# A longer planned latency for the loads of the weight preparation, a wider spread of it, queries' low parts on partitions 0 to 63, and sinks' probabilities moved by small transfers

## The chip, the core and the metric

The kernel runs on one core of a Trainium2 chip. The metric is the time of one execution in microseconds (us). The profile is of one execution and names the engines so: PE is TensorE (PEld its weight loads), DVE is VectorE, ACT is ScalarE, POOL is GpSimd, SP is SyncE, whose queue (SPq) issues nearly all DMAs here. L12 is line 12 of the kernel before.

## What is computed

Sliding-window attention with sink keys, then two feed-forward layers without gating. Everything is float32; a product is made of two or three passes of a faster format on a high and a low part of each number.

```
scores = (1/sqrt(64)) * q @ k.T                 # 4 x 8 heads, 768 positions, 64 wide
keep   = (key < 4) | (0 <= query - key < 128)   # 4 sink keys, a window of 128
a = softmax(where(keep, scores, -1e9));  x = a @ v          # -> 3072 tokens x 512
h = relu(x @ moe_w_in);                  x = (h*h) @ moe_w_out      # 512 -> 2048 -> 512
h = x @ moe2_w_in;  g = h - tanh(h);     out = g @ moe2_w_out
```

## The kernel before

**Tiling and stages.** Attention is done in jobs, one for a head and a block of 384 queries: 8 blocks of 8 heads. The first 16 jobs are done in plain float32 (`plain`), the other 48 in split form (`job`, `scores`, `values`). Layer one (`step1`) runs over 8 token blocks `t` of 384 and 16 slices `n` of the hidden width: `mm_a` makes a slice in bank `ph` or `T`, ReLU and square follow (`r`), a high and a low part (`gh`, `gl`) are made, and `mm_b` adds the slice's share to the four banks `acc`. While layer one works on a block, the attention of the next but one is done between its matmuls. Layer two (`pair2`, `step2`) starts when layer one is over, at about 690 us, and needs its weights in a prepared form.

**The weight preparation** is the third thing that runs beside layer one. `sums` (16 items) and `halves` (16 items) prepare the weights of layer two for later: each loads a piece of `w` into the one buffer `zr`, rebuilds float32 from 64-bit words in the buffer `wd` (`to_single`: rebias L586 on ACT or L588 on DVE, then L591, L593, L595 on DVE), subtracts pieces (L626, L629), splits into a high part (back into `zr`) and a low part (L289, `wd<-wd,zr`), and stores both to DRAM (`wc`, or `wo` for `halves`). The next item's load of `zr` waits for the store of this one. `SUMS` says at which point of layer one, in token blocks, each of the 32 items is due: from 2.0 at steps of 0.13.

**One split job on the engines.** PE makes scores of 128 queries in bank `S` (L345 with the keys' high part, L346 with the low), three times a job; DVE lays the causal half over it (L350) and takes the row's minimum (L411, which frees `S`), ACT takes the exponential (L355). The probabilities are normed (`cb`), those of the sinks split into `ask`, and PE transposes all into bank `O` (L379 three times, L380 for `ask`: for the three groups of queries, 8 rows each stand on partitions 0, 32 and 64). ACT copies the transposed window part to `xe` (high), DVE subtracts (L391, low), POOL cuts it to the window by two selects (L395, `pt`); three small copies of 8x128 bring the sinks' rows from bank `O` to partitions 0 to 7 of `pts`. Then PE multiplies with the values (L431, L434 with `pt`, and last L436 with `pts`), into the same bank `O`; `tmp` and `x` (copy, L447, L449) take the result out.

**Low parts of queries.** The queries of a head stand twice in `raw` and in `qq`, on partitions 0 to 63 and again on 64 to 127 (so do the keys). A copy makes both halves of `qq` high parts; a subtraction (L289, `qq<-raw,qq`, 64x384) then turns the half on partitions 64 to 127 into low parts.

**What sets the order.** No engine's order is written out. Every operation is given to `Order` with the engines that can do it, a cost on each (`C(occupied, took)`; `c_act`, `c_two` and so on), a priority (its due time) and what it reads and writes. `solve` plans all of them, DMAs too (engine `D`, planned in `load` with bytes / 300 ns or at least 430 ns, and 1700 ns until the data are there), and the operations are written down by their planned starts. Each engine then works through its list in that order; an operation whose input is late holds up all that stand behind it on that engine, and SP's queue does likewise. A fixed number of completion semaphores for DMAs is used in turn.

Of the kernel before, what the change touches and what calls it, by code (L numbers as in the profile page):

```python
# [12 lines left out]
F32 = mybir.dt.float32  # L13
F32R = mybir.dt.float32r
# [26 lines left out]

EARLY = 25.0, 8.0
RING = 9
SUMS = tuple(2.0 + i * 0.13 for i in range(32))
LATER = 190.0
NU = NM // 2
NC = 7
REBIAS = 2.0 ** -112
# [185 lines left out]
def c_two(n, psum=False):  # L234

    return C(n / 0.96 + 72, None, not psum)
# [4 lines left out]
    return {"A": c_act(n, psum), "V": c_one(n, psum or apart)}  # L241


def c_pool(n):
    return C(max(2.35 * n + 110, 290.0), None, True)

# [11 lines left out]
class Fast:  # L258
# [30 lines left out]
            (nc.vector if e == "V" else nc.gpsimd).tensor_tensor(out=out, in0=a, in1=b.bitcast(F32), op=ALU.subtract)  # L289
        self.o.add({"V": c_two(n), "P": c_pool(n)}, prio, reads, writes, emit)  # L290

    def load(self, prio, writes, get, nbytes, reads=()):
        nc = self.nc

        def emit(e):
            out, in_ = get()
            nc.sync.dma_start(out=out, in_=in_)
        t = max(nbytes / 300.0, 430.0)
        self.o.add({"D": C(t, t + 1700.0)}, prio, reads, writes, emit)


    def job(self, j, due):

        t = self.t
        blk, head = divmod(j, H)
        b, half = divmod(blk, 2)
        plain = j < PLAIN
        nk, nv, k2 = KW[half], NV[half] - 2 * (not plain), j % 2
        q, r = (j % 4, j % 4) if plain else (k2, k2)
        d = due[0]  # L310
        if j > 1:
            src, early = self.raw[half][b * H + head], 8 * plain
            self.load(d - 24 - early, [("rq", q), ("rk", q)], lambda: (t["raw", q][:, :QW[half]], src[:, :QW[half]]), P * QW[half] * 4)
            self.load(d - 23 - early, [("rv", r)], lambda: (t["rv", r][:, :nv * D], src[:, RW[half] - nv * D:]), P * nv * D * 4)

        def vals():
            return t["rv", r][:, :nv * D].rearrange("p (n d) -> p n d", d=D)
        if plain:
            self.plain(j, half, head, blk, q, due)
            return  # L320
        x = t["raw", q]
        self.copy(d - 16, [("rq", q)], [("qh", k2), ("ql", k2)], lambda: (t["qq", k2], x[:, :N1]), N1)
        self.sub(d - 15, [("rq", q)], [("ql", k2)], lambda: (t["qq", k2][64:], x[64:, :N1], t["qq", k2][64:]), N1)
        self.copy(d - 16, [("rk", q)], [("kh", k2)], lambda: (t["kh", k2][:, :nk], x[:, N1:N1 + nk]), nk)
        self.sub(d - 15, [("rk", q), ("kh", k2)], [("kl", k2)], lambda: (t["kl", k2][:, :nk], x[:, N1:N1 + nk], t["kh", k2][:, :nk]), nk)
        vh, vl = (slice(D, 2 * D), slice(0, D)) if head % 2 == 0 else (slice(0, D), slice(D, 2 * D))
        self.copy(d - 8, [("rv", r)], [("vh", k2)], lambda: (t["vv", k2][:, :nv, vh], vals()), nv * D, apart=True)
        self.sub(d - 7, [("rv", r), ("vh", k2)], [("vl", k2)], lambda: (t["vv", k2][:, :nv, vl], vals(), t["vv", k2][:, :nv, vh]), nv * D)
        self.scores(j, half, due)
        self.values(j, half, head, blk, due[2])  # L330

    def scores(self, j, half, due):
# [59 lines left out]
        for s, sign, op in ((1, 1, ALU.is_ge), (0, -1, ALU.is_gt)):  # L392
            u = 0 if s else i0
            o.add({"P": c_sel(2 * P * (3 - u))}, d - 5, [(*xe, 0), (*xe, 1)], [("pt", 2 * i + s) for i in range(u, 3)],
                  lambda e, u=u, s=s, sign=sign, op=op: nc.gpsimd.affine_select(  # L395
                      out=t[pt].rearrange("p (n t) q -> p n t q", t=2)[:, 2 * u:, s, :], in_=t[xe][:, 2 * u:, :].bitcast(F32),
                      pattern=[[0, 2 * (3 - u)], [sign, P]], compare_op=op, fill=0.0, base=0, channel_multiplier=-sign))
        for i in range(3):
            self.copy(d - 6, [tb], [("pts", k2, i)], lambda i=i: (t["pts", k2][0:8, i * P:(i + 1) * P], bank[tb][32 * i:32 * i + 8, 3 * P:]), P, True)

    @staticmethod
    def keys(half, i):
# [17 lines left out]
    def values(self, j, half, head, blk, d):  # L420
        nc, o, t, bank = self.nc, self.o, self.t, self.bank
        k2, ob = j % 2, ("O", 0)
        wins = self.windows(half)


        def pv(e):
            oo, vv, pt, pts = bank[ob], t["vv", k2], t["pt", 0], t["pts", k2]
            for n, (b, sl, cnt, c) in enumerate(wins):
                k = sl + sl // 2 * 2
                if sl == 5:  # L430
                    nc.tensor.matmul(out=oo[:, c:c + 2 * P], lhsT=vv[:, b - 2, :], rhs=pt[:, k:k + 3:2, :], start=False, stop=False)  # L431
                    continue
                for l in range(2):
                    nc.tensor.matmul(out=oo[:, c:c + cnt * P], lhsT=vv[:, b - 2, :], rhs=pt[:, k + 2 * l:k + 2 * l + 3 * cnt - 2:3, :],  # L434
                                     start=(n == 0 and l == 0), stop=False)
            nc.tensor.matmul(out=oo[:, :N1], lhsT=vv[:, 0, :], rhs=pts, start=False, stop=True)  # L436
        o.add({"T": c_mm(N1, *[256] * (5 + 2 * half))}, d - 4,
              [("vh", k2), ("vl", k2)] + [("pts", k2, i) for i in range(3)] + [("pt", s) for s in range(1 - half, 6)], [ob], pv)

        r, q = (0, 64) if head % 2 == 0 else (64, 0)  # L440

        def at(x, w):
            return t[x, 0][r:r + 64, w]
        own, one, low = slice(0, N1), slice(2 * P, N1), slice(N1, N1 + P)
        self.copy(d - 3, [ob], [("tmp", 0)], lambda: (at("tmp", slice(0, 512)), bank[ob][q:q + 64, :]), 512, True)
        o.add({"V": c_two(N1, True)}, d - 2.5, [ob, ("tmp", 0)], [("x", r)],
              lambda e: nc.vector.tensor_tensor(out=at("x", own), in0=bank[ob][r:r + 64, :N1], in1=at("tmp", own), op=ALU.add))  # L447
        o.add({"V": c_two(P), "P": c_pool(P)}, d - 2.4, [("tmp", 0), ("x", r)], [("x", r)],
              lambda e: (nc.vector if e == "V" else nc.gpsimd).tensor_tensor(out=at("x", one), in0=at("x", one), in1=at("tmp", low), op=ALU.add))  # L449
        self.split(head, blk, d, ("x", 0), [("x", 0), ("x", 64)])  # L450

# [158 lines left out]
    def sums(self, u, kc, prio, after):  # L610
# [7 lines left out]
        rk, zk = ("zr", 0), [("wd", 0), ("wd", 1)]  # L618
        for m, dst in ((u + NU, slice(0, 4, 3)), (u, slice(1, 3))):
            self.load(prio - 6, [(*rk, m // NU)],  # L620
                      lambda m=m, dst=dst: (four[:, dst, :], self.w[1][m, :, :1024].rearrange("p (n c) -> p n c", c=2 * P)[:, kc:4:2, :]), P * 2048, after)
        rks = [(*rk, 0), (*rk, 1)]
        self.to_single(prio, lambda: (raw, z[:, :512]), rks, zk)
        tt = nc.vector.tensor_tensor
# [15 lines left out]
    def halves(self, n, prio, after):  # L640


        raw, z = self.t["zr", 0], self.t["wd", 0]
        rks, zk = [("zr", 0, 0), ("zr", 0, 1)], [("wd", 0), ("wd", 1)]
        m, zf = n // 2 + (1 - n % 2) * NU, z[:, :512].bitcast(F32)
        self.load(prio - 6, rks, lambda: (raw, self.w[1][m, :, 1024:]), P * 4096, after)
        self.to_single(prio, lambda: (raw, z[:, :512]), rks, zk)
        hi, lo = raw[:, :512].bitcast(F32R), z[:, :512].bitcast(F32R)
        self.copy(prio + 0.6, zk, rks, lambda: (hi, zf), 512)
        self.sub(prio + 0.7, zk + rks, zk, lambda: (lo, zf, hi), 512)  # L650
        for i, (src, ks) in enumerate(((hi, rks), (lo, zk))):
            self.load(prio + 0.8, [("wo", n, i)], lambda i=i, src=src: (self.wo[:, n, i * 512:(i + 1) * 512], src.bitcast(F32)), P * 2048, ks)
# [204 lines left out]
    def plan(self):  # L857
# [16 lines left out]
                due = [base(blk) + u * span(blk) - 2.0 for u in us]  # L874
                self.job(blk * H + head, due)

        attn = {"qh", "ql", "kh", "kl", "vh", "vl", "cb", "nm", "ss", "rs", "ask", "xe", "pt", "pts", "tmp", "x"}
        own = [(x, i) for x in ("qh", "ql", "kh", "kl", "vh", "vl", "ss", "rs", "tmp") for i in range(2)] + [("pt", i) for i in range(6)] + [("x", 0), ("x", 64)]
        own += [(x, k, i) for x in ("cb", "nm", "ss", "ask", "xe", "pts") for k in range(2) for i in range(3)]
        attention(0)  # L880
        self.switch(lambda k: k[0] == "wide", [("acc", i) for i in range(4)] + [("ph", 0), ("S", 0)], self.x_wide, self.banks)
# [8 lines left out]
        for q in range(4):  # L890
# [2 lines left out]
                            own, self.x_plain, self.attn)  # L893
            for n in range(8):
                self.step1(q % 2, n + 8 * (q // 2), PV[q] + n * PS[q], q // 2)
            if q > 1:
                attention(q)
        for t in range(2, NB1):
# [32 lines left out]
        for t in range(NB2):  # L931
# [4 lines left out]

    ATTN = (("qq", 2, (N1,), F32R), ("kh", 2, (KW[1],), F32R), ("kl", 2, (KW[1],), F32R), ("vv", 2, (NV[1] - 2, 2 * D), F32R),
            ("cb", 2, (3, 132), F32), ("nm", 2, (3,), F32), ("ss", 2, (3,), F32), ("rs", 2, (3,), F32), ("ask", 2, (96,), F32R),
            ("xe", 1, (6, P), F32R), ("pt", 1, (12, P), F32R), ("pts", 2, (N1,), F32R), ("tmp", 1, (512,), F32), ("x", 1, (N1,), F32))
    PLAINS = (("raw", (2, 3), (QW[1],), F32), ("rv", (2, 3), (NV[1] * D,), F32), ("pcb", 4, (3, 132), F32), ("pnm", 4, (3,), F32), ("pss", 4, (3,), F32),  # L940
              ("prs", 4, (3,), F32), ("pxe", 2, (3, P), F32), ("ppp", 4, (6, P), F32), ("psk", 2, (96,), F32), ("pps", 4, (P,), F32), ("px", 1, (N1,), F32))
    AFTER = (("x2", NC, (1024,), F32R), ("ys", 1, (NE, 2 * P), F32), ("h", 2, (N2,), F32))
# [334 lines left out]
```

## Time and profile before

| | us |
|---|---|
| median of 3 runs | 1230.92 |
| lowest and highest run | 1229.64, 1231.37 |
| time of the profiled execution | 1229.52 |
| span of the profiled execution, first to last instruction | 1227.8 |
| PE busy in it | 1203.4 |
| DVE busy in it | 985.7 |
| ACT busy in it | 888.8 |

The profiled execution lies 1.4 us below the median; its span leaves out 1.7 us of its time. A row of a timeline gives start, duration and, in brackets, how long the engine stood idle before it and what ended that. A row of waits gives who waited for whom, the sum, the number of times and the longest. A matmul's duration is that of its way through the array; matmuls start one behind the other at shorter distances than that.

### The profile page before, as it was taken

The numbers are of one execution on the slowest core, as the hardware profiler recorded it, in microseconds if no ns is written. First come the engines' busy times: TensorE is split into PE (matmuls) and PEld (weight loads), VectorE is DVE, ScalarE is ACT, GpSimd is POOL, SyncE is SP. The second block draws the span as 40 slices with busy tenths as digits, with TensorE's granted clock in tenths as the row PEclk, the third lists the DMA queues.
The fourth block names the chain that finished last, engine by engine and source line by source line (L and its number), as shares of the span: only waits on it lengthen the run. The fifth ranks groups of instructions, "written<-read, shape, count | busy, mean of one in ns | idle before, by whom it ended". The sixth has DMA issues, their size and how long they took to land.

```text
span 1227.8 us, 21601 instructions
## 1 busy us (share of the span) xinstructions
PE 1203.4 (98%) x7434; PEld 1124.2 (92%) x7434; DVE 985.7 (80%) x2248; ACT 888.8 (72%) x2183; POOL 181.5 (15%) x216
## 2 busy tenths in 40 slices
PE   8999999999999999999999999999999999999997
PEld 6889999999999899999899998899998989998995
DVE  8999986978888888888864377887877977977775
ACT  7776875777887788778764466776776877866765
POOL 3321322222221222232220000010100100100000
PEclk9999999999999999999999999999999999999999
DMA  8982231545555555455338775566665665655641
GB/s 285 315 322 74 62 93 53 147 136 166 154 157 176 141 157 184 158 163 167 121 124 269 251 230 174 175 237 189 197 218 186 219 200 158 219 164 175 206 138 37
DMA packets 112312, 214.75 MB, mean 175 GB/s; under 512 B 9282, under 2 KB 67138, under 8 KB 112194
## 3 DMA queue, kind: packets, MB, share of 16 engines
q1 hardware_dynamic: 112050, 212.89, 54.5%
q8 instruction: 60, 0.98, 0.3%
q14 instruction: 58, 0.48, 0.1%
q10 hardware_dynamic: 144, 0.40, 0.1%
HBM read 176.03 MB, written 37.22 MB: 174 GB/s over the span
## 4 chain that ended last, share of the span: by engine, by line
PE 79%; DVE 8%; DMA 6%; ACT 4%; issue 2%; SPq 0%; DVEq 0%; ACTq 0%
PE acc L677 20%; PE acc L675 16%; PE ph L661 11%; PE T L661 6%; PE S L744 5%; PE T L744 5%; PE O L744 4%; PE ph L744 4%; DMA zr<-w 3%; DMA wc<-zr 2%; PE O L434 2%; PE S L345 1%; PE S L346 1%; PE O L379 1%; PE S L479 1%
## 5 line engine op out<-in xcount | busy, mean ns | idle before, releaser
L675 PE MATMUL acc<-gh,w 128*128 128x384 f32 x1024 | 306.9, 339 | 0.5 <-ACT y L276 0.3
L677 PE MATMUL acc<-v,g2h 128*128 128x512 f32 x768 | 259.6, 391 | 0.1
L661 PE MATMUL ph<-xh,w 128*128 128x384 f32 x640 | 215.4, 343 | 2.0 <-DVE r L693 0.8
L675 PEld LDWEIGHTS acc<-gh,w 128*128 128x128 f32 x1024 | 189.1, 188 | 1.6 <-ACT y L276 0.5
L675 PE MATMUL acc<-gl,w 128*128 128x384 f32 x512 | 173.1, 338 | 0.3
L677 PEld LDWEIGHTS acc<-v,g2h 128*128 128x128 f32 x768 | 144.6, 188 | 27.5 <-ACT g2h L276 0.8
L677 PE MATMUL acc<-v,g2l 128*128 128x512 f32 x384 | 151.0, 393 | 0.4 <-DVE g2l L289 0.4
L661 PE MATMUL T<-xh,w 128*128 128x384 f32 x384 | 128.5, 336 | 0.0
L395 POOL TENSOR_SCALAR_AFFINE_SELECT pt<-xe 128x768 fp32r<-128x768 f32 x96 | 89.9, 959 | 239.1 <-DVE xe L391 230.3
L661 PEld LDWEIGHTS ph<-xh,w 128*128 128x128 f32 x640 | 119.8, 188 | 4.7 <-ACT r L691 1.6
L289 DVE TENSOR_TENSOR gl<-r,gh 128x384 fp32r<-128x384 f32 x124 | 77.4, 625 | 46.3 <-ACT gh L276 45.7
L661 PE MATMUL ph<-xl,w 128*128 128x384 f32 x320 | 107.7, 336 | 0.1
L675 PEld LDWEIGHTS acc<-gl,w 128*128 128x128 f32 x512 | 96.3, 188 | 3.4 <-DVE gl L289 2.6
L677 PEld LDWEIGHTS acc<-v,g2l 128*128 128x128 f32 x384 | 72.6, 189 | 11.1 <-DVE g2l L289 1.1
L355 ACT ACTIVATE cb<-cb,nm 128x132 f32<-128x132 f32 x144 | 57.9, 402 | 31.5 <-DVE nm L411 30.6
L661 PEld LDWEIGHTS T<-xh,w 128*128 128x128 f32 x384 | 72.1, 188 | 0.0
L783 ACT ACTIVATE wd<-zr,sqb 128x512 f32<-128x512 f32 x96 | 68.7, 716 | 0.0
L791 DVE TENSOR_TENSOR wd<-wd,h 128x512 f32<-128x512 f32 x96 | 66.3, 691 | 2.8
L787 ACT ACTIVATE mk<-zr,umax 128x512 f32<-128x512 f32 x96 | 68.1, 709 | 0.0
L789 DVE SCALAR_TENSOR_TENSOR wd<-wd,zr 128x512 f32<-128x512 f32 x96 | 66.4, 691 | 1.7 <-ACT wd L783 1.7
L661 PE MATMUL T<-xl,w 128*128 128x384 f32 x192 | 64.5, 336 | 0.0
L780 ACT ACTIVATE zr<-h 128x512 f32<-128x512 f32 x96 | 60.1, 626 | 1.9
(214 smaller groups left out, 2838.7 us busy)
## 6 DMA issues: line engine op xcount, KB each, us to landing
s<-wc SPq DMA_DIRECT2D x168, 512.0 KB, 4.4
wr<-w SPq DMA_DIRECT2D x32, 512.0 KB, 8.0
raw<-raw SPq DMA_DIRECT2D x32, 454.0 KB, 4.1
raw<-raw SPq DMA_DIRECT2D x31, 390.0 KB, 3.5
zr<-w SPq DMA_DIRECT2D x32, 256.0 KB, 3.8
zr<-w SPq DMA_DIRECT2D x16, 512.0 KB, 3.8
v<-wo SPq DMA_DIRECT2D x16, 512.0 KB, 4.7
yd<-y SPq DMA_DIRECT2D x40, 192.0 KB, 2.4
```

The lines of the kernel that those rows point to most:

```text
L289: (nc.vector if e == "V" else nc.gpsimd).tensor_tensor(out=out, in0=a, in1=b.bitcast(F32), op=ALU.subtract)
L355: lambda e, i=i: nc.scalar.activation(out=t[cb][:, i, :], in_=t[cb][:, i, :], func=AF.Exp, bias=t[nm][:, i:i + 1], scale=-1.0, accum_out=t ...
L395: lambda e, u=u, s=s, sign=sign, op=op: nc.gpsimd.affine_select(out=t[pt].rearrange("p (n t) q -> p n t q", t=2)[:, 2 * u:, s, :], in_=t[x ...
L661: nc.tensor.matmul(out=ph[:, :N1], lhsT=w[:, a + c * P:a + (c + 1) * P], rhs=b[:, c, :], start=(c == 0 and k == 0), stop=(c == NE - 1 and ...
L675: nc.tensor.matmul(out=acc[:, :N1], lhsT=w[:, a + e_ * P:a + (e_ + 1) * P], rhs=g, start=st, stop=sp)
L677: nc.tensor.matmul(out=acc, lhsT=g[:, e_ * P:(e_ + 1) * P], rhs=w[:, a:a + 512], start=st, stop=sp)
L744: nc.tensor.matmul(out=out(), lhsT=w[:, off + wo + kc * P:off + wo + (kc + 1) * P], rhs=x[:, xo + kc * 256:xo + (kc + 1) * 256], start=(st ...
L780: o.add({"A": c_act(N2)}, v + 1.5, hs, [u], lambda e: nc.scalar.activation(out=T[u], in_=T[h], func=AF.Square))
L783: lambda e: nc.scalar.activation(out=T[w], in_=T[u], func=AF.Square, scale=SQ_S, bias=self.c["sqb"]))
L787: lambda e: nc.scalar.activation(out=T[mk], in_=T[u], func=AF.Relu, scale=-1.0, bias=self.c["umax"]))
L789: lambda e: nc.vector.scalar_tensor_tensor(out=T[w], in0=T[w], scalar=SQ_D, in1=T[u], op0=ALU.add, op1=ALU.mult))
L791: lambda e: nc.vector.tensor_tensor(out=T[w], in0=T[w], in1=T[h], op=ALU.mult))
```

## The change

Five things are changed:

- `SUMS` starts at 1.7 with steps of 0.145, so the 32 items of the preparation begin 0.3 of a token block earlier and are due up to 6.195 instead of 6.03.
- The loads of `zr` in `sums` and `halves` are planned with 2000 ns more until their data are there (`LATE`). Nothing of the load itself changes.
- The low parts of the queries are made in the half of `qq` on partitions 0 to 63 instead of 64 to 127.
- The sinks' probabilities: one copy of 96x128 from bank `O` to a new buffer `ps` takes the place of the three copies of 8x128, and three DMAs of 4 KB each, SBUF to SBUF, bring the rows from partitions 0, 32 and 64 of `ps` to partitions 0 to 7 of `pts`. They have a priority 80 above their due time.
- The planned costs of `tmp`'s copy, and of L447 and L449 when their rows stand on partitions 64 to 127, go up by 170 and 115 ns (`off`); `tmp`'s copy may now go to ACT alone.

```diff
-SUMS = tuple(2.0 + i * 0.13 for i in range(32))
+SUMS = tuple(1.7 + i * 0.145 for i in range(32))
 LATER = 190.0
+LATE = 2000.0
...
+def off(c, on=True):
+
+    return C(c[0] + 170.0, c[1] + 115.0, c[2]) if on else c
...
-    def load(self, prio, writes, get, nbytes, reads=()):
+    def load(self, prio, writes, get, nbytes, reads=(), late=0.0):
...
-        self.o.add({"D": C(t, t + 1700.0)}, prio, reads, writes, emit)
+        self.o.add({"D": C(t, t + 1700.0 + late)}, prio, reads, writes, emit)
...
-        self.sub(d - 15, [("rq", q)], [("ql", k2)], lambda: (t["qq", k2][64:], x[64:, :N1], t["qq", k2][64:]), N1)
+        self.sub(d - 15, [("rq", q)], [("ql", k2)], lambda: (t["qq", k2][:64], x[:64, :N1], t["qq", k2][:64]), N1)
...
+        ps = ("ps", 0)
+        self.copy(d - 6, [tb], [ps], lambda: (t[ps][:96], bank[tb][:96, 3 * P:]), P, True)
         for i in range(3):
-            self.copy(d - 6, [tb], [("pts", k2, i)], lambda i=i: (t["pts", k2][0:8, i * P:(i + 1) * P], bank[tb][32 * i:32 * i + 8, 3 * P:]), P, True)
+            self.load(d - 80.0, [("pts", k2, i)], lambda i=i: (t["pts", k2].bitcast(F32)[0:8, i * P:(i + 1) * P], t[ps].bitcast(F32)[32 * i:32 * i + 8, :]), 8 * P * 4, [ps])
...
-        self.copy(d - 3, [ob], [("tmp", 0)], lambda: (at("tmp", slice(0, 512)), bank[ob][q:q + 64, :]), 512, True)
-        o.add({"V": c_two(N1, True)}, d - 2.5, [ob, ("tmp", 0)], [("x", r)],
+        o.add({"A": off(c_act(512, True))}, d - 3, [ob], [("tmp", 0)],
+              lambda e: nc.scalar.copy(out=at("tmp", slice(0, 512)), in_=bank[ob][q:q + 64, :]))
+        o.add({"V": off(c_two(N1, True), r)}, d - 2.5, [ob, ("tmp", 0)], [("x", r)],
...
-        o.add({"V": c_two(P), "P": c_pool(P)}, d - 2.4, [("tmp", 0), ("x", r)], [("x", r)],
+        o.add({"V": off(c_two(P), r), "P": c_pool(P)}, d - 2.4, [("tmp", 0), ("x", r)], [("x", r)],
...
+                for i, at in enumerate(SUMS):
+                    if at < 2.0 and q == 3 and int((at - 1.5) * NM) == n:
+                        self.sums(i // 2, i % 2, V0 + at * TB, [("step", 1, n + 8)])
```

Both loads of `zr` get `LATE` as their last argument.

PE's list is the same up to the first split jobs and again from the start of layer two; between them 1570 of its 5934 rows stand elsewhere. DVE, around the end of the third item of the preparation and the start of the fourth, before (`L289 wd<-wd,zr` ends an item, `L588` is the first operation on the newly loaded `zr`):

```order
L289 TENSOR_TENSOR wd_184<-wd_184,zr_185 128x896
L289 TENSOR_TENSOR qq_1216<-raw,qq_1216 64x384
...
L391 TENSOR_TENSOR xe_1233<-O_62,xe_1233 128x3x128
L588 TENSOR_SCALAR wd_184<-zr_185 128x512
L350 COPY_PREDICATED S_453<-up,S_453 128x128
L591 TENSOR_SCALAR wd_184<-wd_184 128x512
L411 ISA cb_1223,nm_1225<-S_453,m_79 128x132
```

And in the changed kernel (L295, L597, L356, L600 and L419 are L289, L588, L350, L591 and L411 of before):

```order
L295 TENSOR_TENSOR wd_184<-wd_184,zr_185 128x896
L397 TENSOR_TENSOR xe_1233<-O_62,xe_1233 128x3x128
...
L708 TENSOR_TENSOR r_176<-r_176 128x384
L597 TENSOR_SCALAR wd_184<-zr_185 128x512
L397 TENSOR_TENSOR xe_1233<-O_62,xe_1233 128x3x128
L600 TENSOR_SCALAR wd_184<-wd_184 128x512
L356 COPY_PREDICATED S_453<-up,S_453 128x128
L419 ISA cb_1223,nm_1225<-S_453,m_79 128x132
```

Between the two items stand 15 rows of other work before and 21 now; over the 31 such places the mean is 14.7 before and 18.1 now.

SP's queue, around the stores and the next load of one item of the preparation, before:

```order
L297 DMA raw<-raw 128x780
L297 DMA raw<-raw 128x256
L297 DMA wc<-zr_185 128x7x128
L297 DMA wc<-wd_184 128x7x128
L297 DMA zr_185<-w 128x2x256 x2
L297 DMA raw<-raw 128x908
L297 DMA raw<-raw 128x256
```

And in the changed kernel, around a like place:

```order
L303 DMA wc<-wd_184 128x7x128
L303 DMA pts_1235<-ps_1237 8x128 x3
L303 DMA zr_185<-w 128x2x256 x2
L303 DMA raw<-raw 128x908
L303 DMA raw<-raw 128x320
L303 DMA pts_1236<-ps_1237 8x128 x3
L303 DMA wc<-zr_185 128x7x128
```

The 48 triples stand in 51 groups (some are split by another DMA); 25 of the groups stand directly behind a load of `raw`, 10 behind one of `zr`, 16 behind a store.

ACT, at one job's transposed probabilities, before:

```order
L276 CAST xh_190<-x_1238 128x384
L276 COPY y_183<-acc_449 128x384
L276 CAST xe_1233<-O_62 128x3x128
L276 CAST pts_1235<-O_62 8x128 x3
L276 CAST qq_1216<-raw 128x384
```

And in the changed kernel:

```order
L282 CAST xh_190<-x_1239 128x384
L361 ACTIVATE cb_1224,ss_1228<-cb_1224,nm_1226 128x132
L282 CAST xe_1233<-O_62 128x3x128
L282 CAST ps_1237<-O_62 96x128
L361 ACTIVATE cb_1224,ss_1228<-cb_1224,nm_1226 128x132
```

The three copies have become one, which stands directly behind that of `xe`.

## Rows read from the trace of the kernel before

**Rows 1.** The page, busy time of each engine, its share, its instructions.
```profile
PE 1203.4 (98%) x7434; PEld 1124.2 (92%) x7434; DVE 985.7 (80%) x2248; ACT 888.8 (72%) x2183; POOL 181.5 (15%) x216
```

**Rows 2.** Stages: window, length, busy us of each engine, PE clock, DMA share, GB/s.
```profile
200.00:450.00 250.00, 242.90 (x1486) 236.14 (x1485) 211.26 (x560) 191.37 (x545) 57.88 (x66) 1.00 0.52 150
...
580.00:640.00 60.00, 58.39 (x356) 56.12 (x355) 45.72 (x119) 42.53 (x120) 15.98 (x19) 1.00 0.34 115
640.00:1200.00 560.00, 559.28 (x3479) 511.99 (x3478) 417.53 (x688) 391.27 (x767) 14.66 (x9) 1.00 0.62 199
```

**Rows 3.** Waits of PE from 200 to 640 us: sum, times, longest.
```profile
PE S L345 <- DVE nm L411: 5.9, 9, 1.9
PE O L434 <- POOL pt L395: 0.8, 1, 0.8
PE ph L661 <- DVE r L693: 0.8, 2, 0.4
PE O L379 <- DVE x L447: 0.6, 1, 0.6
```

**Rows 4.** The chain that ended last, from 260 to 275 us: start, duration, what.
```profile
262.20 4.90 DMA wc<-zr
...
267.53 4.41 DMA zr<-w
...
272.06 0.06 DVE wd L588
...
273.29 0.39 PE S L345
```

**Rows 5.** Waits of DVE, over the whole span.
```profile
DVE wd L588 <- DMA zr<-w: 15.8, 14, 3.1
```

**Rows 6.** DMA issues: count, KB each, median us from issue to landing.
```profile
zr<-w SPq DMA_DIRECT2D x32, 256.0 KB, 3.8
...
wo<-zr SPq DMA_DIRECT2D x16, 256.0 KB, 2.0
...
raw<-raw SPq DMA_DIRECT2D x24, 128.0 KB, 2.9
```

**Rows 7.** Timeline of ACT at 303 us, and copies of `pps` from its tile's view.
```profile
303.53 0.79 ACT L276 CAST pts<-O 8x128 fp32r<-8x128 f32 x3
...
L276 ACT COPY pps<-T x13: 259/265/284, 13.2 to 87.3; 96x128 f32<-96x128 f32 x13
```

**Rows 8.** Timeline of DVE at 309 us, around one subtraction of `qq`.
```profile
309.10 0.28 DVE L411 CUSTOM_DVE_ANT_0 cb<-S,m 128x132 f32<-128x132 f32 x1
309.31 0.08 DVE L411 DVE_READ_ACCUMULATOR2_ANT nm<- 128x1 f32 x1
309.42 0.55 DVE L289 TENSOR_TENSOR qq<-raw,qq 64x384 fp32r<-64x384 f32 x1
310.01 1.09 DVE L289 TENSOR_TENSOR wd<-wd,zr 128x896 fp32r<-128x896 f32 x1
```

**Rows 9.** Timeline from 334 us: one job from its transposes to its values.
```profile
334.32 0.30 PE L380 MATMUL O<-idr,ask 128*96 128x128 f32 x1
...
335.08 0.46 ACT L276 CAST xe<-O 128x384 fp32r<-128x384 f32 x1
335.44 0.25 ACT L276 CAST pts<-O 8x128 fp32r<-8x128 f32 x1
...
336.64 2.30 POOL L395 TENSOR_SCALAR_AFFINE_SELECT pt<-xe 128x768 fp32r<-128x768 f32 x2 [4.17 <-DVE xe L391]
...
339.47 0.39 PE L434 MATMUL O<-pt,vv 128*128 128x256 f32 x2
```

**Rows 10.** The chain that ended last: nine matmuls of 384 columns in a row.
```profile
126.37 1.56 PE acc L675 x9
```

**Rows 11.** View of the tile `zr`: ns min/median/max, first and last start.
```profile
L780 ACT ACTIVATE zr<-h x96: 614/632/637, 695.9 to 1210.9; 128x512 f32<-128x512 f32 x96
...
L297 SPq DMA_DIRECT2D wo<-zr x16: 319/326/327, 471.8 to 634.1; - x16
```

More of the change, by code (lines that the diff above doesn't have):

```diff
@@ L620, in sums @@
             self.load(prio - 6, [(*rk, m // NU)],
-                      lambda m=m, dst=dst: (four[:, dst, :], self.w[1][m, :, :1024].rearrange("p (n c) -> p n c", c=2 * P)[:, kc:4:2, :]), P * 2048, after)
+                      lambda m=m, dst=dst: (four[:, dst, :], self.w[1][m, :, :1024].rearrange("p (n c) -> p n c", c=2 * P)[:, kc:4:2, :]), P * 2048, after, LATE)
         rks = [(*rk, 0), (*rk, 1)]
@@ L645, in halves @@
         m, zf = n // 2 + (1 - n % 2) * NU, z[:, :512].bitcast(F32)
-        self.load(prio - 6, rks, lambda: (raw, self.w[1][m, :, 1024:]), P * 4096, after)
+        self.load(prio - 6, rks, lambda: (raw, self.w[1][m, :, 1024:]), P * 4096, after, LATE)
         self.to_single(prio, lambda: (raw, z[:, :512]), rks, zk)
@@ L875, in attention @@
                 self.job(blk * H + head, due)
-        attn = {"qh", "ql", "kh", "kl", "vh", "vl", "cb", "nm", "ss", "rs", "ask", "xe", "pt", "pts", "tmp", "x"}
-        own = [(x, i) for x in ("qh", "ql", "kh", "kl", "vh", "vl", "ss", "rs", "tmp") for i in range(2)] + [("pt", i) for i in range(6)] + [("x", 0), ("x", 64)]
+        attn = {"qh", "ql", "kh", "kl", "vh", "vl", "cb", "nm", "ss", "rs", "ask", "xe", "pt", "pts", "ps", "tmp", "x"}
+        own = [(x, i) for x in ("qh", "ql", "kh", "kl", "vh", "vl", "ss", "rs", "tmp") for i in range(2)] + [("pt", i) for i in range(6)] + [("x", 0), ("x", 64), ("ps", 0)]
         own += [(x, k, i) for x in ("cb", "nm", "ss", "ask", "xe", "pts") for k in range(2) for i in range(3)]
@@ L938 @@
             ("cb", 2, (3, 132), F32), ("nm", 2, (3,), F32), ("ss", 2, (3,), F32), ("rs", 2, (3,), F32), ("ask", 2, (96,), F32R),
-            ("xe", 1, (6, P), F32R), ("pt", 1, (12, P), F32R), ("pts", 2, (N1,), F32R), ("tmp", 1, (512,), F32), ("x", 1, (N1,), F32))
+            ("xe", 1, (6, P), F32R), ("pt", 1, (12, P), F32R), ("pts", 2, (N1,), F32R), ("ps", 1, (P,), F32R), ("tmp", 1, (512,), F32), ("x", 1, (N1,), F32))
     PLAINS = (("raw", (2, 3), (QW[1],), F32), ("rv", (2, 3), (NV[1] * D,), F32), ("pcb", 4, (3, 132), F32), ("pnm", 4, (3,), F32), ("pss", 4, (3,), F32),
```

## The prediction

> **What bounds the kernel now.** I read the busy times first: PE works 1203.4 us of a span of 1227.8 [rows 1], so the most that any change off PE can give back is PE's idle time, and the question is where that lies. The stages say it [rows 2]: from 200 to 450 us PE is busy 242.90 of 250 (7.1 us idle), from 580 to 640 us 58.39 of 60 (1.6 idle), and from 640 to 1200 us only 0.7 us is idle. Between 200 and 640 us three jobs run side by side: layer one, the split attention and the weight preparation. There lie 8.8 us of idle time that this change can reach; the start (before the first split job) and layer two keep their order.
>
> Who is waited for there [rows 3]: 5.9 us, nine times, a score matmul waits for bank `S`, which DVE's minimum L411 has not left yet; 0.8 us for POOL's select; 0.8 us for a ReLU on DVE; 0.6 us for L447. DVE is 85% busy in the same stage (211.26 of 250, rows 2), so it isn't full. It is held up, and the chain of waits shows by what [rows 4]: the store of one item of the preparation takes 4.90 us, the load of `zr` behind it lands 4.41 us after its issue has begun, at 272 us L588 starts on it, and only behind L588 in DVE's list stands the minimum that PE waits for; PE goes on at 273.29. DVE stands before L588 waiting for `zr` 14 times and 15.8 us in all [rows 5]. So PE's idle time is mostly a load that comes later than the plan thought, passed on by an engine that works in order.
>
> **The change part by part.**
>
> *The planned latency and the wider spread.* A load of `zr` is planned at 256 KB / 300 + 1700 = 2.57 us; the rows say 3.8 at the median [rows 6], and two of them stand one behind the other. In the case of [rows 4] the second was planned to land 3.45 us after the first was issued (874 ns more), and the store before it at 3.2 us; measured were 4.8 (267.1 to 271.94) and 4.90, together 3.1 us late, and DVE stood for about that long. With 2.0 us more planned, the plan puts other work ahead of L588: between two items stand on average 18.1 rows of DVE in place of 14.7 (the order shows 21 in place of 15 at this spot); at some 0.5 us each that is 1.7 us. PE's longest wait was 1.9 us [rows 3], so what 2 us of other work covers is nearly all of it. The waits that I put down to `zr` are the minimum's 5.9, the select's 0.8 and L447's 0.6: 7.3 us. I take 6.0, since at the latest loads 1 us remains; bounds 2 and 7.3. What could be lost: the preparation ends later, by the order of DVE at the 111th low part `gl` in place of the 105th of 124, some 28 us. The last store from `zr` was at 634 us and layer two takes the buffer at 696 [rows 11], so 62 us cover it; were that gone, each us over it would be one of PE's.
>
> *Low parts on partitions 0 to 63.* In DVE's timeline each operation starts shortly before the one ahead has ended (309.31 against 309.10 + 0.28), but the subtraction of `qq` starts 0.03 after and the next one 0.04 after it [rows 8]. What is saved per job is the overlap on both sides, about 0.2 us, and 48 jobs give 10 us of DVE over 500 us. DVE isn't the bound, so on PE this is worth a share of the ReLU's 0.8 us [rows 3]: 0.5, bounds 0 and 0.8.
>
> *One copy in place of three.* Three copies of 8x128 take 0.79 us on ACT and one of 96x128 0.265 (`pps`, the same shape) [rows 7]: 0.5 us a job, 25 us of ACT in all, which is 77% busy (rows 2). PE's only waits on ACT are under half a us. I take 0.3, bounds 0 and 0.5.
>
> *The three DMAs.* This is the part that can cost. Nothing in the trace moves 4 KB from SBUF to SBUF. The path of a job [rows 9]: transposes issued by 334.46 (0.14 after L380's start), `xe` copied from 335.08, then the small copies from 335.44, POOL's selects from 336.64 for 2.3, values at 339.47. With one copy of 0.265 in place of the first small one, the third DMA starts at about 335.71 + 0.05 + 2 x 0.35 = 336.46, that is 2.0 us behind the transposes; if it lands L later, PE can go on at 2.0 + L. Meanwhile PE has other matmuls in its list. Counted in the new order, at 1.56 / 9 = 0.173 us for one of 384 columns [rows 10], they last 4.27 us at the shortest and 5.29 at the mean of the 48 jobs (4.03 and 4.87 before). With L = 2.0, the store of 256 KB from `zr`, no job waits; with L = 2.9, the load of 128 KB, the smallest here [rows 6], 16 jobs wait, 4.9 us in all. I take the middle, 2.4 us: the source is SBUF as in the store and the size 1/32, but 35 of 51 groups stand directly behind a load on SP's queue. POOL's selects, which end at about 338.9, hide a landing of 2.5 us anyhow. A gain from this part is excluded, since the copies it replaces were counted above. What is queued behind a triple on SP are loads for later jobs, which have whole jobs to spare; what can hold it up is a load ahead of it that waits for a buffer.
>
> The Trainium skill (DMA: Bandwidth & Descriptors, Anatomy of one DMA) gives a fixed 2.0 us for a DMA, most of it the receipt from the memory written, heaviest for DRAM. By that, as an estimate, the triples would cost nothing and the sum would be 2.4 us lower; I keep the value from the rows, because the page's fit has no other traffic in it.
>
> *Planned costs of `tmp`, L447, L449* change no duration; 47 of 48 copies of `tmp` were on ACT already. I cost them at nothing.
>
> **The sum.** 6.0 + 0.5 + 0.3 - 2.4 = 4.4 us less. The profiled execution took 1229.52, so 1225.1; it lies 1.4 below the median of 1230.92, so the median to expect is 1226.5.
>
> **The rivals.**
>
> *Late triples (slower).* The 35 groups behind a load land when that load's own data do, since the same queue carries both: then L is not 2.0 to 2.9 but about 3.8, as for `zr` [rows 6]. At 3.8 all 48 jobs would lose 31 us, 35 of 51 groups 21 us; less the gains of 6.8 that is 14 us slower, 1245. It decides from L of about 3.0 at all jobs, where the loss reaches 6.8. For it: the DMA engines are 52% busy in this stage (rows 2). Against it: 4 KB, and the loads ahead are mostly issued well before. Milder forms, a triple held up now and then by a `raw` load that waits for DVE, give 1231 to 1236.
> The Trainium skill has a rule for it (same page, Queues, rings and completion order): one queue's descriptors are taken up in ring order on each DMA engine. No row of this trace shows a small transfer behind a large one.
>
> *No change.* DVE's wait for `zr` goes, but another late input takes its place: ReLU banks or transposes that the plan now packs just as tightly, since it plans again with the time it thinks it has. Then 2 us of the first part remain, the triples take them back, and the time is 1229 to 1231. For it: DVE and ACT are each 77 to 85% busy and their lists are newly mixed (1570 of PE's rows moved). Against it: the freed 10 us of DVE and 25 of ACT are real slack, and the preparation is spread over 88 such slices of layer one in place of 75.
>
> *More than forecast.* All 8.8 us of idle time between 200 and 640 us go, and with them the 0.1 us by which the first matmul after each of some 15 gaps is longer (1.5 us): 1220.5. It needs triples that cost nothing.
>
> **How the numbers follow.** A measurement of this kernel tells 0.2%, 2.5 us, from no change. The forecast (1223 to 1228.4) has 0.42, more than forecast (1219.5 to 1223) 0.14, no change (1228.4 to 1233.4) 0.22, slower 0.22, of which the milder forms up to 1237 have 0.12 and the late triples 0.10. Faster is then 0.56. The range from 1219.5 to 1235 leaves out the late triples, part of the milder forms and little else, some 0.17. Of the likeliest case alone it would be 1223 to 1228.4.
>
> **What would show it.** In the profile of the changed kernel DVE's waits for `zr` before the rebias should fall from 15.8 us to under 6, and PE's waits for the minimum from 5.9 to under 2. `qq`'s subtraction should overlap with its neighbours. ACT should be about 25 us less busy. The triples should land 2 to 2.9 us after issue, and PE's waits for `pts` before the last matmul of a job's values should stay under 5 us. The prediction is wrong if PE waits at L431, L434 or L436 for 10 us or more (then it is the landing or SP's queue, and the view of SP's waits tells which), or if the waits for the minimum stay though those for `zr` have gone.

## The result and the profile after

The changed kernel takes 1214.39 us at the median of 4 runs (1213.52 to 1214.91), the kernel before 1230.28 in the runs of the same comparison. The ratio is 0.9872, with a 95% interval from 0.9851 to 0.9892: 16 us faster, where 4 were forecast and 11 were the end of the range. The profiled execution took 1214.91, with a span of 1213.2. The sign and the place were right; the size was not.

The numbers of the lines have moved: L345, L411, L588, L675 and L677 of before are L351, L419, L597, L684 and L686 of after. Busy times of the kernel after, from its page, to be held against [rows 1]:

```profile
PE 1197.4 (99%) x7434; PEld 1125.3 (93%) x7434; DVE 982.6 (81%) x2247; ACT 869.5 (72%) x2096; POOL 184.3 (15%) x212
```

PE's idle time has fallen from 24.4 (1227.8 - 1203.4) to 15.8 us, which is 8.6 us, but the span by 14.6. The other 6 us went out of PE's busy time, though PE runs the same 7434 matmuls. The stages show it too (kernel after; columns as in [rows 2]):

```profile
200.00:450.00 250.00, 249.32 (x1559) 248.15 (x1558) 215.43 (x578) 189.61 (x528) 69.88 (x74) 1.00 0.53 154
450.00:580.00 130.00, 129.79 (x809) 128.86 (x809) 108.95 (x298) 95.21 (x267) 28.64 (x34) 1.00 0.49 154
580.00:640.00 60.00, 60.00 (x370) 59.93 (x369) 41.79 (x104) 40.05 (x103) 9.61 (x11) 1.00 0.40 131
```

Between 200 and 450 us PE now starts 1559 matmuls and before 1486 [rows 2]. At 250 / 1559 = 0.16 us each, the 73 more are worth 11.7 us; the busy time of the same window rose by only 6.4.

**Where the rest had been.** A row of PE lasts longer than the distance to the next one, so a PE that starts nothing still shows as busy for a while. These are PE and its weight loads (PEld) in the kernel before, at the gap of [rows 4] and at a place where no idle time of PE is shown:

```profile
208.44 0.34 PE L675 MATMUL acc<-gh,w 128*128 128x384 f32 x1
208.91 0.19 PEld L675 LDWEIGHTS acc<-gl,w 128*128 128x128 f32 x1 [0.46 <-DVE gl L289]
208.91 0.45 PE L675 MATMUL acc<-gl,w 128*128 128x384 f32 x1
...
271.03 0.34 PE L661 MATMUL T<-xh,w 128*128 128x384 f32 x1
273.29 0.19 PEld L345 LDWEIGHTS S<-kh,qq 128*128 128x128 f32 x1 [2.24 <-DVE nm L411]
273.29 0.39 PE L345 MATMUL S<-kh,qq 128*128 128x260 f32 x1 [1.93 <-DVE nm L411]
```

At 208.44 the next matmul starts 0.47 us later in place of 0.173 [rows 10]: 0.30 lost. Of this 0.13 is idle time (the first row ends at 208.78), too short for the row to show it, and 0.17 counts as busy. The weight load names the wait, and with 0.46 puts it 0.16 higher than what is lost. At 271.03 the loss is 2.26 - 0.17 = 2.09; PE's row gives 1.93. Waits of PEld from 100 to 690 us (columns as in [rows 3]), first before, then after:

```profile
PEld S L345 <- DVE nm L411: 9.2, 10, 2.2
PEld acc L675 <- DVE gl L289: 2.6, 8, 0.5
PEld O L434 <- POOL pt L395: 2.2, 5, 1.1
PEld ph L661 <- DVE r L693: 1.3, 2, 0.6
PEld O L379 <- DVE x L447: 1.0, 2, 0.8
PEld acc L675 <- ACT y L276: 0.5, 1, 0.5
PEld ph L661 <- ACT r L691: 0.5, 2, 0.3
PEld ph L661 <- DVE xl L289: 0.4, 1, 0.4
PEld O L380 <- DVE ask L289: 0.2, 1, 0.2
```

```profile
PEld O L442 <- POOL pt L401: 1.3, 2, 0.7
PEld acc L684 <- DVE gl L295: 1.3, 3, 0.6
PEld ph L670 <- ACT r L700: 0.5, 1, 0.5
PEld S L351 <- DVE nm L419: 0.2, 1, 0.2
```

They add up to 17.9 and 3.3 us. The difference, 14.6, is that of the spans. That it fits so well is partly luck: each wait counts some 0.15 us too much, and waits of under 0.2 us aren't listed. The starts of all matmuls in the two traces tell it without this. Each distance held against the median for the same two matmuls (over six of the kernels below), stalls of over 0.2 us took 12.0 us before and 2.2 after between 100 and 690 us, and those of 0.05 to 0.2 us 8.7 and 4.4. And where `zr` was waited for [rows 5], DVE after the change waits 1.0 us in place of 15.8:

```profile
DVE wd L597 <- DMA zr<-w: 1.0, 2, 0.8
```

### The profile page after: what moved, and what is told of

It is laid out like the page before. It is cut to its first block, busy times and chain, and to the rows that moved or that the text cites. A ratio compares the mean times of both kernels' runs of the same rounds, so it can differ in the third digit from the quotient of the medians.

```text
span 1213.2 us, 21754 instructions
## 1 busy us (share of the span) xinstructions
PE 1197.4 (99%) x7434; PEld 1125.3 (93%) x7434; DVE 982.6 (81%) x2247; ACT 869.5 (72%) x2096; POOL 184.3 (15%) x212
## 4 chain that ended last, share of the span: by engine, by line
PE 88%; DVE 5%; ACT 3%; issue 1%; DMA 1%; POOL 1%; SPq 0%; DVEq 0%; ACTq 0%; POOLq 0%
PE acc L686 20%; PE acc L684 20%; PE ph L670 12%; PE T L670 7%; PE S L753 6%; PE T L753 5%; PE O L753 4%; PE ph L753 4%; PE O L442 2%; PE S L352 1%; PE S L351 1%; PE O L385 1%; PE S L488 1%; PE O L444 1%; ACT pcb L506 1%
## 5 line engine op out<-in xcount | busy, mean ns | idle before, releaser
L684 PE MATMUL acc<-gh,w 128*128 128x384 f32 x1024 | 309.0, 339 | 0.2 <-DVE w L295 0.2
L686 PE MATMUL acc<-v,g2h 128*128 128x512 f32 x768 | 259.7, 391 | 0.1
L684 PEld LDWEIGHTS acc<-gh,w 128*128 128x128 f32 x1024 | 189.1, 188 | 1.1 <-DVE w L295 0.5
L684 PE MATMUL acc<-gl,w 128*128 128x384 f32 x512 | 172.4, 337 | 0.5 <-DVE gl L295 0.3
L686 PEld LDWEIGHTS acc<-v,g2h 128*128 128x128 f32 x768 | 144.7, 188 | 27.5 <-ACT g2h L282 0.8
L686 PE MATMUL acc<-v,g2l 128*128 128x512 f32 x384 | 151.1, 393 | 0.5 <-DVE g2l L295 0.5
L401 POOL TENSOR_SCALAR_AFFINE_SELECT pt<-xe 128x768 fp32r<-128x768 f32 x96 | 96.7, 1031 | 229.6 <-DVE xe L397 216.4
L295 DVE TENSOR_TENSOR gl<-r,gh 128x384 fp32r<-128x384 f32 x122 | 74.3, 609 | 56.5 <-ACT gh L282 55.4
L684 PEld LDWEIGHTS acc<-gl,w 128*128 128x128 f32 x512 | 96.3, 188 | 2.5 <-DVE gl L295 2.0
L686 PEld LDWEIGHTS acc<-v,g2l 128*128 128x128 f32 x384 | 72.6, 189 | 11.1 <-DVE g2l L295 1.1
L700 ACT ACTIVATE r<-ph 128x384 f32<-128x384 f32 x72 | 35.3, 490 | 42.6 <-PE ph L670 42.0
```

The lines of the kernel that those rows point to most:

```text
L684: nc.tensor.matmul(out=acc[:, :N1], lhsT=w[:, a + e_ * P:a + (e_ + 1) * P], rhs=g, start=st, stop=sp)
L686: nc.tensor.matmul(out=acc, lhsT=g[:, e_ * P:(e_ + 1) * P], rhs=w[:, a:a + 512], start=st, stop=sp)
L700: nc.scalar.activation(out=r, in_=ph, func=AF.Relu)
```

## The experiments

Two questions are open after this: which of the five parts does it, and whether the plan's parts work by themselves or through the relief of DVE and ACT. Kernels named b_ are the kernel before with parts of the change, those named a_ the changed kernel without one part or with another number. Ratios are to the kernel before, on the same chip, with the 95% interval.

### One part at a time

**b_qq**: the low parts alone. The plan doesn't know the partition, so every order stays.

```diff
-... (t["qq", k2][64:], x[64:, :N1], t["qq", k2][64:]), N1)
+... (t["qq", k2][:64], x[:64, :N1], t["qq", k2][:64]), N1)
```

> The kernel before with the low parts of the queries on partitions 0 to 63 and nothing else; the plan's costs don't know the partition, so the order of every engine is that of before. Theory A (late loads: the 16 us come from planning the loads of zr later and spreading them): at most 1 us less, DVE's subtraction of qq overlaps with its neighbours, PE's weight loads still wait some 9 us for the minimum. Theory B (slack: the 16 us come from DVE and ACT being relieved, 10 us and 25 us): 3 to 6 us less from this part alone. Theory C (any new plan moves the time by several us): no change, since the plan is the same.

Measured: 0.9994 (0.9979 to 1.0009), no change. DVE did get what was counted on; its timeline in this kernel, against [rows 8]:

```profile
308.83 0.54 DVE L289 TENSOR_TENSOR qq<-raw,qq 64x384 fp32r<-64x384 f32 x1
309.31 1.07 DVE L289 TENSOR_TENSOR wd<-wd,zr 128x896 fp32r<-128x896 f32 x1
```

The next operation starts 0.06 us before the subtraction ends, where it started 0.04 after. DVE still stands 16.5 us before `zr`, PE's weight loads 8.7 for the minimum (200 to 640 us): what DVE saves, it then waits.

**b_late**: the 2000 ns alone.

```diff
+LATE = 2000.0
-        self.o.add({"D": C(t, t + 1700.0)}, prio, reads, writes, emit)
+        self.o.add({"D": C(t, t + 1700.0 + late)}, prio, reads, writes, emit)
```

> The kernel before with 2000 ns more planned for the loads of zr, due times as before. Theory A: 8 to 14 us less; DVE's waits for zr fall from 15.8 us to under 5 and the waits of PE's weight loads for the minimum from 9.2 to under 3. Theory B: at most 4 us less, since DVE and ACT have as much to do as before. Theory C: a few us either way, without relation to DVE's waits for zr.

Measured: 0.9946 (0.9928 to 0.9964), 6.6 us, less than the 8 of theory A. DVE's waits for `zr` are gone, those of PE's weight loads (100 to 690 us) only in part:

```profile
DVE wd L589 <- DMA zr<-w: 0.9, 1, 0.9
```

```profile
PEld S L346 <- DVE nm L412: 6.1, 13, 1.3
PEld acc L676 <- DVE gl L290: 2.1, 5, 0.8
PEld acc L676 <- ACT y L277: 0.9, 1, 0.9
```

The longest wait for the minimum has gone from 2.2 to 1.3 us, but there are 13 now in place of 10. So A by this part alone is only half of it: the late loads made the long stops, and something else makes short ones.

**b_ps**: the one copy and the three DMAs alone.

> The kernel before with the sinks' probabilities copied once to ps and moved by three DMAs a job, nothing else. Theory A: between 2 us less and 5 us more, since DVE still stands before late loads; the loads of zr stand behind more DMAs on SP's queue and may come later still. Theory B: 4 to 8 us less, with ACT about 25 us less busy. Theory C: a few us either way.

Measured: 1.0006 (0.9993 to 1.002), no change, though ACT is 22 us less busy (866.8 against 888.8). B falls with this and with b_qq, as a cause by itself. Some 2000 of PE's 7434 matmuls stand elsewhere than before here, and the time didn't move, which speaks against C.

**b_shift**: due times at steps of 0.1305, a control.

> The kernel before with the due times of the preparation's items at steps of 0.1305 of a token block in place of 0.13, which does nothing but make the plan come out a little differently. Theories A and B: within 2 us of before. Theory C: 3 us or more away from before, either way.

Measured: 0.9996 (0.998 to 1.0012). As a test of C this says nothing: in its trace PE's matmuls and ACT's operations stand in the same order as before and two of DVE's 2254 rows elsewhere, so the plan hardly came out otherwise. What it shows is how closely a kernel with nearly the same order repeats. Against C stand b_ps above and a_no_late below, two plans with some 2000 matmuls moved and times within 0.2% of before; for parts worth a few us C isn't excluded.

**b_off**: the raised planned costs alone.

```diff
-        self.copy(d - 3, [ob], [("tmp", 0)], ..., 512, True)
-        o.add({"V": c_two(N1, True)}, d - 2.5, ...
+        o.add({"A": off(c_act(512, True))}, d - 3, ...
+        o.add({"V": off(c_two(N1, True), r)}, d - 2.5, ...
```

> The kernel before with the raised planned costs of tmp's copy, L447 and L449 alone. Theory E: 2 to 8 us less. Theory F: within 2.5 us of before, with DVE's waits for zr still over 10 us.

Measured: 0.9963 (0.9952 to 0.9974), 4.6 us, by an edit that makes no instruction shorter (it also bars `tmp`'s copy from DVE, which made one of 48 before). DVE still waits 9.9 us for `zr`, just under the 10 that F set. The profile doesn't show where the 4.6 us are: PE's weight loads wait 18.7 us in all and 17.9 before, and the last matmul starts at 1219.9 us and at 1220.1 before.

### One part taken out

**a_no_late**: `LATE = 0.0` in the changed kernel.

> The changed kernel with the loads of zr planned as before (no 2000 ns more), the other parts kept. Theory A (late loads carry most of the 16 us, the plan's extra 2 us alone gave 6.5): 6 to 12 us more than the changed kernel, 1220 to 1227, with DVE waiting 10 us or more for zr. Theory D (the parts work together, each taking away waits that another leaves): 3 to 8 us more. If the wider spread alone were enough: within 2 us of the changed kernel.

Measured: 0.9985 (0.9973 to 0.9996), that is 1230 us: nearly the whole gain is gone, with every other part in place, more than A's 12 us and D's 8. DVE's waits for `zr` are back to the number and the sum of before, and PE's weight loads wait 18.4 us in all, 7.1 of it for the minimum:

```profile
DVE wd L597 <- DMA zr<-w: 15.7, 14, 2.4
```

```profile
PEld S L351 <- DVE nm L419: 7.1, 13, 1.6
PEld acc L684 <- ACT y L282: 4.7, 3, 2.2
```

**a_no_sums, a_no_qq, a_no_ps**: due times, low parts, sinks' copies as before.

> The changed kernel with the due times of the 32 items as before (2.0 and steps of 0.13). Theory A: 2 to 5 us more than the changed kernel, because with DVE 85% busy or more the items crowd it and PE's weight loads wait 4 to 6 us for the minimum, as in the kernel with the planned latency alone. Theory D: 1 to 4 us more.

> The changed kernel with the queries' low parts on partitions 64 to 127 again; the order of every engine stays that of the changed kernel. Theory A: within 1 us of the changed kernel, as on the kernel before. Theory D: 2 to 4 us more, since without the late loads DVE's own pace is what PE's minimum waits for, and DVE then has up to 10 us more to do.

> The changed kernel with the three small copies of the sinks' probabilities in place of one copy and three DMAs. Theory A: within 2 us of the changed kernel, either way. Theory D: 2 to 5 us more, with ACT some 25 us busier and PE waiting for ReLU and selects.

Measured: 0.9868 (0.9851 to 0.9884), 0.986 (0.9843 to 0.9876) and 0.9877 (0.986 to 0.9893), each within its interval of the 0.9872 of the whole change. None of the three is needed as long as the other two are there. D's losses came in none of them, nor did A's for the wider spread. In a_no_sums PE waited for a triple, once:

```profile
PEld O L444 <- DMA pts<-ps: 0.6, 1, 0.6
```

**a_no_off**: planned costs as before.

> The changed kernel with the planned costs of tmp's copy, L447 and L449 as before (and tmp's copy again open to DVE). Theory E (costs that were planned too low are the second cause: what operations on partitions 64 to 127 hold up made DVE run behind its plan): 5 to 9 us more than the changed kernel, with PE's weight loads waiting some 5 us or more for the minimum. Theory F (behind the planned load, any one of the other parts gives enough slack): within 2.5 us of the changed kernel.

Measured: 0.9916 (0.9894 to 0.9938): 0.0044 or 5.4 us of the gain are gone. PE's weight loads wait 7.4 us from 100 to 690 us, 2.1 of it for the minimum from 200 to 640, so E's size was met and its share of the minimum was not.

### Two and three parts together

**b_late_off** and **b_late_sums**: the 2000 ns with the raised costs, and with the wider spread.

> The kernel before with the 2000 ns and the raised planned costs, nothing else. Theory E: 12 to 15 us less than before (1217 to 1220). Theory F: somewhere between the 6.5 us of the 2000 ns alone and 15 us.

> The kernel before with the 2000 ns and the wider spread of the items, nothing else. Theory E: 6 to 9 us less than before, hardly more than the 2000 ns alone. Theory F: 11 to 15 us less, and PE's weight loads wait under 2 us for the minimum.

Measured: 0.9919 (0.9897 to 0.994) and 0.9909 (0.9887 to 0.9931), 10 and 11 us. Both come out above the 6.6, though their intervals touch that of b_late, and neither brings the whole; E's 12 us are missed, and of F's two signs for b_late_sums the time is met and the wait is not (3.9 us for the minimum). b_late_off differs from a_no_sums only in the low parts and the transfers. Those two together, which did nothing by themselves, take it from 0.9919 to 0.9868, 6 us, with intervals that lie apart; the waits of PE's weight loads fall from 8.2 to 2.7 us. On top of b_late_sums the same two bring nothing (a_no_off, 0.9916).

**b_late_off_sums**: the three parts that only change the plan.

> The kernel before with the three parts that only change the plan: 2000 ns more for the loads of zr, the wider spread and the raised planned costs; low parts on partitions 64 to 127 and small copies as before. Theory E (plan alone): within 3 us of the changed kernel, 1214 to 1218, PE's weight loads waiting under 6 us between 100 and 690 us. Theory G (the relief of DVE and ACT is needed too): 1219 or more.

Measured: 0.9885 (0.9857 to 0.9914), 14 us of the 16. PE's weight loads wait 10.0 us, where E wanted under 6. The interval holds the 0.9872 of the whole, so whether the low parts and the transfers add the last 1 to 2 us, and with it E or G, stays open. Together with b_late_off it says that the planned latency and the raised costs need one thing more, the spread or the relief by low parts and transfers, and that either will do for most of the rest.

**a_late1** and **a_late4**: 1000 and 4000 ns in the changed kernel.

> The changed kernel with 1000 ns more planned for the loads of zr in place of 2000. If the gain follows the loads' real lateness (the two largest were 2.3 to 3.1 us behind the old plan, most 1 to 2): between the two, 1217 to 1224, DVE waiting 3 to 9 us for zr. If any shift of the plan will do: within 2 us of the changed kernel.

> The changed kernel with 4000 ns planned in place of 2000. If the gain follows the loads' real lateness: no further gain, 1213 to 1217, since DVE waits 1.0 us for zr already; the preparation only ends later. If the plan profits from every further delay: 1211 or less.

Measured: 0.99 (0.9878 to 0.9923) with DVE waiting 6.1 us for `zr`, between the two as the loads' lateness says; and 1.0192 (1.0171 to 1.0214) with 4000, 24 us slower than before, which neither theory had. There the preparation ends too late. PE's longest wait from 600 to 800 us, and the tile `zr` (columns as in [rows 11]), in a_late4:

```profile
PE acc L686 <- ACT g2h L282: 28.3, 1, 28.3
```

```profile
L789 ACT ACTIVATE zr<-h x96: 614/632/643, 737.6 to 1236.9; 128x512 f32<-128x512 f32 x96
...
L303 SPq DMA_DIRECT2D wo<-zr x16: 319/320/378, 510.6 to 737.7; - x16
```

And in the changed kernel:

```profile
L789 ACT ACTIVATE zr<-h x96: 614/632/637, 681.3 to 1197.4; 128x512 f32<-128x512 f32 x96
...
L303 SPq DMA_DIRECT2D wo<-zr x16: 319/327/373, 466.2 to 655.2; - x16
```

Layer two takes the buffer over where the last store is issued: at 737 us with 4000 ns, with PE standing 28.3 us. With 2000 ns the last store is at 655.2 and layer two begins at 681.3, which leaves 26 us of the 62 of before. Layer one is slower too with 4000 ns: PE's weight loads wait 8.1 us there in place of 3.3.

### All kernels in one table

Profiled executions; the sum of PEld's waits is that of the view from 100 to 690 us.

| kernel | ratio | profiled us | DVE waits for `zr` | PEld waits | us less PEld waits |
|---|---|---|---|---|---|
| before | 1 | 1229.5 | 15.8 | 17.9 | 1211.6 |
| b_qq | 0.9994 | 1231.3 | 16.5 | 19.4 | 1211.9 |
| b_ps | 1.0006 | 1232.5 | 11.9 | 20.6 | 1211.9 |
| b_shift | 0.9996 | 1228.7 | 13.5 | 16.8 | 1211.9 |
| b_off | 0.9963 | 1227.6 | 9.9 | 18.7 | 1208.9 |
| a_no_late | 0.9985 | 1229.7 | 15.7 | 18.4 | 1211.2 |
| b_late | 0.9946 | 1223.3 | 0.9 | 10.8 | 1212.5 |
| b_late_off | 0.9919 | 1222.4 | 2.6 | 8.2 | 1214.2 |
| b_late_sums | 0.9909 | 1222.5 | none listed | 11.1 | 1211.4 |
| b_late_off_sums | 0.9885 | 1221.1 | 1.4 | 10.0 | 1211.1 |
| a_late1 | 0.99 | 1221.0 | 6.1 | 8.7 | 1212.3 |
| a_no_off | 0.9916 | 1220.0 | 3.7 | 7.4 | 1212.6 |
| a_no_ps | 0.9877 | 1215.5 | 1.7 | 5.8 | 1209.7 |
| a_no_sums | 0.9868 | 1216.6 | 1.6 | 2.7 | 1213.9 |
| a_no_qq | 0.986 | 1216.2 | 0.3 | 3.7 | 1212.5 |
| after | 0.9872 | 1214.9 | 1.0 | 3.3 | 1211.6 |
| a_late4 | 1.0192 | 1254.4 | 0.7 | 8.1 | 1246.3 |

Less the waits of PE's weight loads, all but a_late4, which stands still later, come to 1209 to 1214 us. So these waits carry most of the 15 us between before and after. They don't decide between kernels that lie within the 5 us of that spread: b_off waits longer than before and was measured faster, and b_late_sums waits as long as b_late. Each profile is one execution, and that of before took 1229.5 us where its medians were 1230.3 to 1233.1.

## Why the prediction was wrong in size

**The ceiling.** The step that failed is the first: "there lie 8.8 us of idle time that this change can reach". The span lost 14.6 us, so more was within reach. By the starts of the matmuls, what was lost in stalls of over 0.05 us was some 21 us between 100 and 690 us, of which PE's own idle time shows only what lies past the modelled end of the matmul ahead. A stall of under 0.16 us doesn't show at all, and from each longer one about that much is left out. The prediction added 1.5 us for longer first matmuls and so had the sign of this, not the size. The Trainium skill (Perfetto Trace Analysis, Tensor Engine Instruction) says that the profiler works out a matmul's end from its size and doesn't see it. No row here shows how the end is found; that a matmul is given 0.34 us where its neighbour can start after 0.173 is in line with it.

**The planned latency and the spread.** Forecast 6.0 of 7.3. The mechanism was right: in the changed kernel the DVE waits for `zr` fell from 15.8 to 1.0 us (forecast: under 6), and the waits for the minimum from 5.9 to none in PE's rows (forecast: under 2). The term was mis-sized: the two together gave 11.2 us on the kernel before, and without the 2000 ns the changed kernel loses 13.9 of its 15.7 us (0.9985 against 0.9872).

**The planned costs.** "I cost them at nothing", because they change no duration. This step was wrong too: without them 5.4 us are lost, and PE's weight loads wait 7.4 us in place of 3.3. The plan had held these operations for cheaper than they are. These are DVE's rows of the kernel before around L447, first with its result on partitions 64 to 127 (a job of an odd head), then on 0 to 63:

```profile
229.93 0.70 DVE L289 TENSOR_TENSOR kl<-raw,kh 128x524 fp32r<-128x524 f32 x1
230.66 0.56 DVE L447 TENSOR_TENSOR x<-O,tmp 64x384 f32<-64x384 f32 x1
231.25 0.56 DVE L699 TENSOR_TENSOR r<-r 128x384 f32<-128x384 f32 x1
...
350.57 0.28 DVE L629 TENSOR_TENSOR wd<-wd 128x128 f32<-128x128 f32 x1
350.77 0.54 DVE L447 TENSOR_TENSOR x<-O,tmp 64x384 f32<-64x384 f32 x1
351.24 0.54 DVE L699 TENSOR_TENSOR r<-r 128x384 f32<-128x384 f32 x1
```

The next operation starts 0.59 us after L447 in the one case and 0.47 in the other, and L447 itself starts 0.03 us after the end of the one ahead in place of 0.08 before it: 0.23 us more in all. The plan before had 384 / 0.96 + 72 = 472 ns for both; the change adds 170 for the first. So the raised number is nearer to what the trace shows. That a plan which believes an operation over too early puts the next one, and PE's, too close behind is argued from this. What the 4.6 us of b_off are stays open: there the minimum is still waited for 10.7 us (in b_late_off only 1.3), and beside the other three parts but without the 2000 ns (a_no_late) 1.8 us are left of it.

**Low parts.** Forecast 0.5 us. The overlap came as counted, and the time didn't move, on the kernel before or on the changed one; what it is worth beside the transfers where the spread is missing (6 us for both) wasn't measured by itself. The Trainium skill (VectorE: DVE Perf Modes, Two Vector instructions with no wait between them) states that a VectorE instruction is held until all earlier ones are done if an operand starts in another group of 32 partitions than the last one in that memory; [rows 8] and the rows of b_qq agree, with 0.04 us after and 0.06 us before the end.

**One copy in place of three, and the DMAs.** Forecast 0.3 gained and 2.4 lost; measured together within 0.2% (b_ps, a_no_ps). The 2.4 were mis-sized: nothing was lost. ACT is 19 us less busy, not 25. The path was longer than counted: a small DMA holds SP's queue for 0.63 us and not 0.35, so the third starts 1.3 us after the first and not 0.7. Still PE never waited for `pts` in the changed kernel (POOL did once, 2.7 us). In its job at 316 us the triple is issued from 316.82 on, and the last product, which needs it, starts at 321.56 behind POOL's selects:

```profile
316.53 0.27 ACT L282 CAST ps<-O 96x128 fp32r<-96x128 f32 x1
316.82 2.00 SPq L303 DMA_DIRECT2D pts<-ps  x3
...
318.13 1.62 POOL L401 TENSOR_SCALAR_AFFINE_SELECT pt<-xe 128x768 fp32r<-128x768 f32 x2 [3.54 <-DVE xe L397]
...
321.56 0.34 PE L444 MATMUL O<-pts,vv 128*128 128x384 f32 x1
```

How long a triple takes to land is read from the records of its DMA packets. In this job the last packet of the third transfer ends 2.7 us after the first issue and 1.4 after its own; the median of the 98 of 144 transfers whose packets can be told apart is 1.37. The prediction had 2.4 in its place, and by its own count no job waits at 2.0. Its 2.0 us from the Trainium skill (DMA: Bandwidth & Descriptors, Anatomy of one DMA) are a fit for transfers that GpSimd issues, and these are SP's; the trace shows less.

**The rivals.** Late triples came singly and cost nothing: behind two loads of `zr` and two of `raw`, the triple issued at 327.96 us has its last packet 3.8 us after, and yet PE waited for one only twice in all these kernels, 0.6 us in a_no_sums and 0.2 in a_no_late. No change fell too: nothing of the size of DVE's waits took their place. "More than forecast" was the right one, and its bound was too high, 1220.5, for the reason given first. The cover of 62 us was named, and a_late4 uses it up. Its price of one us of PE for each us over it isn't borne out: layer two takes the buffer 56 us later than in the changed kernel (737.6 against 681.3), PE stands 28.3 us, and the kernel is 40 us longer.

## What to carry to other kernels

Take the time that TensorE loses from the distances between the starts of its matmuls, or from the waits of its weight loads, and not from its idle time: between 100 and 690 us the idle time was 8.8 us here, the waits of the weight loads 17.9, and 14.6 us could be won. In a kernel whose order comes from a plan, an input planned too early costs more than its own wait, since all that stands behind it on that engine is late; here planning it by its measured lateness was worth 6.6 us alone and making DVE or ACT faster alone nothing (b_qq, b_ps). Planning it later still moved the end of its stage into the next: the change gained 16 us with 2000 ns and lost 24 with 4000. And a control has to be looked at too: b_shift was meant as another plan and had nearly the same order.

## What the runs showed of the hardware

SP's DMAs in the changed kernel, from the view of line L303 (ns min/median/max of what the queue is held, first and last start):

```profile
L303 SPq DMA_DIRECT2D s<-wc x168: 319/320/911, 638.5 to 1175.5; - x168
L303 SPq DMA_DIRECT2D pts<-ps x144: 624/631/1022, 120.2 to 620.6; - x144
```

A DMA of 8 rows of 512 bytes holds SP's queue for 0.63 us, twice as long as one of 512 KB over 128 partitions (`s<-wc`, 0.32). Three of them take 2.0 us of the queue, for 12 KB. With little ahead of it such a transfer is complete 1.37 us after its issue has begun; behind the loads at 327.96 us the third of a triple took 2.4.

In a_late4 PE started nothing from 716 to 744.7 us. The granted clock was 1.00 from 690 to 710 us, 0.50 (1.2 GHz) from 720 to 750, and 1.00 again from 750 to 760.
